# A planner that charges every load for the DMA queue, and weight clamps that GpSimd may take

## The chip, the cores and the metric

The kernel runs on one core of a Trainium2 chip. The metric is device time in microseconds (us), the median of several executions. A profile of one execution shows, for each engine, what it did and what it waited for: PE is TensorE's matmul side, PEld its weight loads, DVE is VectorE, ACT is ScalarE, POOL is GpSimd, and SP is SyncE, whose queue issues all of this kernel's loads and stores.

## The reference

Sliding-window attention for 8 batches of 8 heads (576 positions, head size 64, window 64) feeds an RWKV channel mix.

```python
scores = where(0 <= i - j < 64, (q @ k.T) / 8, -1e9)
x      = softmax(scores) @ v                       # heads side by side: (8, 576, 512)
xp     = x shifted by one position
xk, xr = mu_k*x + (1-mu_k)*xp, mu_r*x + (1-mu_r)*xp
k      = maximum(xk @ w_k, 0);  v = (k*k) @ w_v    # w_k 512x1024, w_v 1024x512
out    = sigmoid(xr @ w_r) * v                     # w_r 512x512
```

The three weight matrices arrive as 64-bit floats; x, q, k and v are 32-bit.

## The kernel before, in words

The 4608 rows (8 batches of 576 positions) are cut into 9 units u of 512 rows, and each unit has 4 attention groups, one for each pair of heads. Group g runs in three bursts on PE: `scores` (16 matmuls, which the trace records as 32), `flip` (8 transposes of the softmax weights) and `values` (16 matmuls, 32 in the trace). Between them stand, on other engines: `least` (DVE, 8 masked row minima per group), `exp` (ACT, 8), `shares` (DVE, the reciprocal row sums, tile `rs`), `scale` (four GpSimd instructions or one DVE instruction for each half), and copies out of PSUM (tiles `pt`, `xT`).

A unit's channel mix takes the 4 `xT` tiles. `mix` makes blends (DVE or ACT, tile `d`) and splits each into a high and a low part (tile `xs`; the low part by POOL or DVE). Then PE runs r units (48 matmuls `bank<-xs,ws`), k units (96 more of the same name) and v units (96 matmuls `bank<-ks,ws`). A product of two split numbers takes three matmuls of 128x512.

Before unit 0 can run, the weights are decoded: 20 chunks of 128x512 (4 of w_r, then 8 of w_k, then 8 of w_v). Each chunk takes one `sign` (ACT, `wt<-w`), one `clamp` (`wt<-wt`), three integer steps on DVE, `shift` (`bank<-wt`), `top` (`bank<-w,bank`) and `low` (`wt<-w,bank`), then `first_part` (ACT, `ws<-wt`) and `second_part` (POOL or DVE, `ws<-wt,ws`).

The order of all instructions is set at build time. Every step is a `Piece` with a key, a cost in ns, the pieces it needs, the buffers that it takes and one or more engines. `play` plays the pieces through by these costs: a free engine begins the ready piece with the lowest key. A piece is ready when what it needs is done and, on another engine, a further `lag` has passed. The order in which pieces begin is the order in which instructions are written out. On the chip each engine then runs its own list strictly in that order and waits wherever data are late. So the costs are never times of the run; they decide only the order.

`transfer` makes the piece of a load. At the start 38 loads without a `key` of their own are recorded: q, k and v of groups 0 to 3, the 20 weight chunks and the two mix vectors. They get a `lag` that grows with the bytes recorded so far. The loads of groups 4 and on have a key and a fixed `lag` of 2000 ns. Each transfer costs SP 60 ns in the play, however many DMAs it issues. Groups 2 and 3 hold their q and k in one tile `qks`, group 3 its v in `vs`.

Line 69 of the kernel is a helper that records every operation, so nearly all rows of the profile carry L69; the tiles tell the steps apart.

Of the kernel before, what the change touches and what calls it, by code (L numbers as in the profile page):

```python
# [14 lines left out]
ALU = mybir.AluOpType  # L15
PSUM = bass.MemoryType.PSUM

P = 128
# [6 lines left out]
UB = 8  # L25
NU = B * NB // UB
TU = UB * W
# [16 lines left out]
LINK = 80  # L44

HI_MIN = struct.unpack("<f", struct.pack("<I", 0x38000000))[0]
HI_MAX = struct.unpack("<f", struct.pack("<I", 0x47EFFE00))[0]
# [3 lines left out]
def attn_rwkv_kernel(ctx, tc, qT, kT, v2, mu_k, mu_r, w_k, w_v, w_r, out):  # L51
# [9 lines left out]
    class Engine:  # L61


        def __init__(self, engine):
            self.engine = engine
# [5 lines left out]
    pe, dve, sca, pool, dma = (Engine(e) for e in (nc.tensor, nc.vector, nc.scalar, nc.gpsimd, nc.sync))  # L71
    room = {"tmp": TB, "bank": 8, "m": 4, "bits": 1, "s": 2, "t": 2, "x": 1, "pr": 4, "sums": 4, "pt": 4, "xT": XB,
            "xs": SB, "r": R_BUFS, "qk": 2, "v": 3}
    pieces = []
# [7 lines left out]
    class Piece:  # L82


        def __init__(self, engine, key, cost, fn, needs=(), takes=(), uses=(), lag=LINK, spare=0, port=False):
            self.costs = engine if isinstance(engine, dict) else {engine: cost}
            self.home = next(iter(self.costs))
            self.engine, self.key, self.fn = None, key, fn
            self.needs = [p for p in needs if p is not None]
            self.takes, self.uses, self.lag, self.spare, self.port = list(takes), list(uses), lag, spare, port  # L90
            for hold in (*self.takes, *self.uses):
                hold.users.append(self)
            self.done = None
            pieces.append(self)

    def play():

        left, free, now, begun, port = {}, {}, 0, [], 0
        for n, p in enumerate(pieces):
            for e in p.costs:  # L100
                left.setdefault(e, []).append((p.key, n, p))
                free[e] = 0
        for e in left:
            left[e].sort(key=lambda x: (x[2].home != e, *x[:2]))
        users = {id(h): len(h.users) for p in pieces for h in p.takes}
        ends = []
        times = [0]
        while any(left.values()):
            assert times, [(e, [(p.key, p.fn.__name__) for _, _, p in ps[:4]]) for e, ps in left.items()]
            now = heapq.heappop(times)  # L110
            while ends and ends[0][0] <= now:
                _, _, p = heapq.heappop(ends)
                for hold in (*p.takes, *p.uses):
                    users[id(hold)] -= 1
                    if not users[id(hold)]:
                        room[hold.tag] += 1
            for e, ps in left.items():
                if free[e] > now:
                    continue
                for _, n, p in ps:  # L120
                    if not all(q.done is not None and q.done + (q.lag if q.engine != e else 30) <= now for q in p.needs):
                        continue
                    tags = [h.tag for h in p.takes]
                    if any(room[tag] < tags.count(tag) + (p.spare if tag == "m" else 0) for tag in set(tags)):
                        continue
                    locks = e == "POOL" or (e == "DVE" and p.port)
                    if locks and port > now:
                        continue
                    if p.home != e and max(free[p.home], now) + p.costs[p.home] < now + p.costs[e]:
                        continue  # L130
                    for o in p.costs:
                        left[o].remove((p.key, n, p))
                    for tag in tags:
                        room[tag] -= 1
                    p.engine = e
                    free[e] = p.done = now + p.costs[e]
                    if locks:
                        port = p.done
                    begun.append(p)
                    for at in (p.done, p.done + 30, p.done + p.lag):  # L140
                        heapq.heappush(times, at)
                    heapq.heappush(ends, (p.done + p.lag, n, p))
                    break
        return begun
# [5 lines left out]
        return 150 + 0.52 * n  # L150

    def act_ns(n):
        return 95 + 0.86 * n

    def pool_ns(n):
        return 195 + 2.1 * n
# [1 line left out]
    engines = {"DVE": dve, "POOL": pool}  # L158
# [63 lines left out]
    def decode(n, loaded):  # L222
        ws, _, i, c = chunks[n]
        key = DECODE[n]
        word, bits = Hold("tmp"), [Hold("bank"), Hold("bits")]

        def sign(e):
            words[n] = tmp.tile([P, WC], F32, name="wt", tag="tmp", bufs=TB)
            sca.activation(words[n], raw[n][:, :, 1].bitcast(F32), AF.Abs)

        def clamp(e):
            dve.tensor_scalar(words[n], words[n], HI_MIN, HI_MAX, op0=ALU.max, op1=ALU.min)

        def shift(e):
            words[n, 0] = bank(WC).bitcast(U32)
            dve.tensor_scalar(words[n, 0], words[n].bitcast(U32), 3, 0x3FFFFFF8,
                              op0=ALU.logical_shift_left, op1=ALU.bitwise_and)

        def top(e):
            dve.scalar_tensor_tensor(words[n, 0], raw[n][:, :, 1], 0xC0000000, words[n, 0],  # L240
                                     op0=ALU.bitwise_and, op1=ALU.bitwise_or)

        def low(e):
            dve.scalar_tensor_tensor(words[n].bitcast(U32), raw[n][:, :, 0], 29, words[n, 0],
                                     op0=ALU.logical_shift_right, op1=ALU.bitwise_or)

        def first_part(e):
            ws[i, c] = const.tile([P, 2, WC], F32R, name="ws", tag="w", bufs=len(chunks))
            sca.copy(ws[i, c][:, 0], words[n])

        def second_part(e):
            engines[e].tensor_sub(ws[i, c][:, 1], words[n], ws[i, c][:, 0].bitcast(F32))

        p = Piece("ACT", key, 600, sign, [loaded], takes=[word])
        p = Piece("DVE", key, 430, clamp, [p], port=True)
        p = Piece("DVE", key, 700, shift, [p], takes=bits)
        p = Piece("DVE", key, 700, top, [p])
        p = Piece("DVE", key, 700, low, [p], uses=bits)
        p0 = Piece("ACT", key, 560, first_part, [p])
        decoded[id(ws), i, c] = p0, Piece({"POOL": 1270, "DVE": 700}, key, 0, second_part, [p0], uses=[word], port=True)  # L260


    loaded, arrived, held = {}, {}, {}
    bus = [0]

    def transfer(fn, size, takes=(), needs=(), key=None):

        p = Piece("SP", len(pieces) - 9999 if key is None else key, 60, fn, needs, takes, lag=2000)
        if key is None:
            bus[0] = max(bus[0], 1300) + size / 300  # L270
            p.lag = bus[0] + 900
        return p


    groups = [(u, c) for u in range(NU) for c in range(NC)]
# [29 lines left out]
    def load_qk(g, key=None):  # L305
        u, c = groups[g]
        held[g] = [Hold("xs" if g in (2, 3) else "qk")]

        def load(e):
            if g in (2, 3):  # L310
                both = act.tile([P, 2, TU], F32, name="qks", tag="xs", bufs=SB)
                loaded[g] = [both[:, 0], both[:, 1]]
            else:
                loaded[g] = [ld.tile([P, TU], F32, name="q"), ld.tile([P, TU + 2 * W], F32, name="k")]
            q, k = loaded[g]
            for b, k0, k1, o in key_loads[u]:
                dma.dma_start(k[:, o * W:(o + k1 - k0) * W], kT[b * NP + c, :, k0 * W:k1 * W])
            o = 0
            for b, i0, i1 in stretches(u):
                n = i1 + 1 - i0  # L320
                dma.dma_start(q[:, o * W:(o + n) * W], qT[b * NP + c, :, i0 * W:(i1 + 1) * W])
                o += n

        arrived[g] = transfer(load, 4 * P * 2 * TU, held[g], key=key)

    def load_v(g, key=None):
        u, c = groups[g]
        held["v", g] = [Hold("xs" if g == 3 else "v")]

        def load(e):  # L330
            if g == 3:
                loaded["v", g] = act.tile([P, UB, P], F32, name="vs", tag="xs", bufs=SB)
            else:
                loaded["v", g] = ld.tile([P, UB, P], F32, name="v", bufs=3)
            for b, a, c0, c1, o in value_loads[u]:
                dma.dma_start(loaded["v", g][:, o:o + c1 - c0], v2[b * NP + c, :, a, c0:c1])

        arrived["v", g] = transfer(load, 4 * P * P * UB, held["v", g], key=key)

    banks, weights, sums, flipped = {}, {}, {}, {}  # L340
    xTs, got = {}, {}
# [316 lines left out]
    load_v(1)  # L658
    load_w(1)
    load_qk(3)  # L660
    arrived["mu"] = Piece("DVE", -25, 300, rest, [transfer(vectors, 4096)])
    load_v(2)
    load_w(1)
    load_v(3)
# [74 lines left out]
```

## Time and profile before

| What | Value |
| --- | --- |
| Median of 3 runs | 698.28 us (697.8 to 699.03) |
| The profiled execution | 697.61 us, of which the span is 695.8 us |
| PE busy | 633.5 us, 91% of the span |
| DVE busy | 413.8 us, 59% |
| ACT busy | 415.6 us, 60% |
| POOL busy | 112.8 us, 16% |
| Granted TensorE clock | 0.989 of full speed |

Shares of busy time are means over stages that differ much. The span has a start of some 130 us, in which weights are decoded and the first groups run, and a long part after it in which PE hardly ever waits. A step of the start is to be read in the start.

### The profile page before, as it was taken

Reading aid. Unit: us, or ns where it says so; the run is one execution under the profiler, and the core shown is the slowest. Engines: PE = TensorE matmul, PEld = TensorE weight load, DVE = VectorE, ACT = ScalarE, POOL = GpSimd, SP = SyncE. Lnnn points to the kernel's source line nnn. Section 1 sums busy time; section 2 is a strip of 40 time slices with the busy share of each in tenths; the row PEclk is TensorE's granted clock in tenths of the full one; section 3 lists DMA queues with packets and bytes.
Section 4 is the critical chain, followed back from the end, with each engine's and each line's share of the span. In section 5 each row is a group of like instructions: output and inputs, shape, how many; then the busy total and the mean of one; then the engine's idle time right before and its main releaser. Section 6 shows DMA issues by size and latency. Waiting matters only on the chain.

```text
span 695.8 us, 12937 instructions
## 1 busy us (share of the span) xinstructions
PE 633.5 (91%) x4752; PEld 510.0 (73%) x4752; DVE 413.8 (59%) x1194; ACT 415.6 (60%) x1130; POOL 112.8 (16%) x183
## 2 busy tenths in 40 slices
PE   1058687899999999999999999999999999999997
PEld 0036565787788888888888888888888888888886
DVE  1047999968758556754675467646764676353311
ACT  2049866947887368646754775477647764671540
POOL 2027784520001000200020002000200020000000
PEclk9998999999999999999999999999999999999999
DMA  8952200244122222222122123222322230001001
GB/s 316 401 183 84 56 1 0 72 151 134 59 60 90 90 60 59 90 90 61 59 90 90 60 59 105 76 65 65 114 80 71 67 112 29 1 16 45 1 0 61
DMA packets 47583, 57.87 MB, mean 83 GB/s; under 512 B 7584, under 2 KB 39328, under 8 KB 47520
## 3 DMA queue, kind: packets, MB, share of 16 engines
q1 hardware_dynamic: 47520, 57.04, 25.4%
q8 instruction: 38, 0.62, 0.4%
q14 instruction: 25, 0.20, 0.1%
HBM read 47.58 MB, written 9.44 MB: 82 GB/s over the span
## 4 chain that ended last, share of the span: by engine, by line
PE 79%; DVE 8%; DMA 5%; ACT 3%; issue 2%; POOL 1%; SPq 0%; DVEq 0%
PE bank L69 79%; DVE bank L69 3%; DVE wt L69 2%; DMA w<-w_v 2%; ACT pr L69 1%; DVE pr L69 1%; DMA q<-qT 1%; DMA w<-w_k 1%; DMA qks<-qT 1%; DMA v<-v 1%; DVE d L69 1%; POOL pr L69 1%; DVE r L69 1%; SPq L69 0%; ACT d L69 0%
## 5 line engine op out<-in xcount | busy, mean ns | idle before, releaser
L69 PE MATMUL bank<-xs,ws 128*128 128x512 f32 x1296 | 316.5, 400 | 9.3 <-ACT xs L69 3.5
L69 PEld LDWEIGHTS bank<-xs,ws 128*128 128x128 f32 x1296 | 244.1, 190 | 68.6 <-ACT xs L69 4.7
L69 PE MATMUL bank<-ks,ws 128*128 128x512 f32 x864 | 209.1, 396 | 1.7 <-ACT xT L69 1.7
L69 PEld LDWEIGHTS bank<-ks,ws 128*128 128x128 f32 x864 | 161.6, 188 | 38.8 <-ACT xT L69 2.1
L69 ACT ACTIVATE pr<-pr,nmax 128x128 f32<-128x128 f32 x288 | 111.9, 393 | 42.5 <-DVE nmax L69 42.4
L69 DVE TENSOR_TENSOR ks<-kf,ks 128x512 fp32r<-128x512 f32 x66 | 45.6, 692 | 82.3 <-ACT ks L69 81.0
L69 PE MATMUL bank<-k,q 64*64 64x128 f32 x1088 | 41.5, 289 | 40.0 <-DMA q<-qT 39.4
L69 ACT ACTIVATE kf<-bank 128x512 f32<-128x512 f32 x72 | 43.0, 599 | 48.6 <-PE bank L69 45.9
L69 PEld LDWEIGHTS bank<-k,q 64*64 64x64 f32 x1088 | 32.4, 140 | 52.3 <-DMA q<-qT 35.8
L69 ACT COPY xT<-bank 128x512 f32<-128x512 f32 x35 | 20.6, 588 | 77.0 <-PE bank L69 76.9
L69 DVE SCALAR_TENSOR_TENSOR r<-bank,r 128x512 f32<-128x512 f32 x36 | 24.9, 692 | 60.7 <-PE bank L69 60.6
L69 DVE CUSTOM_DVE_ANT_0 pr<-bank,maskNone 128x128 f32<-128x128 f32 x224 | 53.7, 286 | 10.5 <-PE bank L69 10.5
L69 ACT ACTIVATE th<-bank 128x512 f32<-128x512 f32 x36 | 21.5, 598 | 63.7 <-PE bank L69 59.6
L69 POOL TENSOR_SCALAR pr<-pr,rs 128x128 f32<-128x128 f32 x76 | 31.8, 437 | 162.8 <-ACT d L69 90.9
L69 ACT ACTIVATION_READ_ACCUMULATOR pr<-pr,nmax 128x1 f32 x288 | 54.9, 191 | 0.0
L69 POOL TENSOR_TENSOR kf<-kf 128x512 f32<-128x512 f32 x12 | 12.5, 1041 | 253.9 <-ACT kf L69 253.9
L69 PE MATMUL bank<-ident,pr 128*128 128x128 f32 x288 | 44.1, 290 | 6.1 <-POOL pr L69 3.3
L69 ACT CAST xs<-d 128x512 fp32r<-128x512 f32 x72 | 43.8, 618 | 3.7 <-DVE d L69 1.6
L69 ACT CAST ks<-kf 128x512 fp32r<-128x512 f32 x72 | 44.2, 617 | 1.7
L69 DVE CUSTOM_DVE_ANT_0 pr<-bank,mask 128x128 f32<-128x128 f32 x64 | 17.9, 286 | 44.3 <-PE bank L69 44.3
L69 PEld LDWEIGHTS bank<-pt,v 128*64 128x64 f32 x1120 | 37.2, 142 | 8.2 <-issue 5.5
L69 PE MATMUL bank<-pt,v 128*64 128x64 f32 x1120 | 42.3, 230 | 1.0 <-ACT kf L69 0.5
(54 smaller groups left out, 585.3 us busy)
## 6 DMA issues: line engine op xcount, KB each, us to landing
v<-v SPq DMA_DIRECT2D x31, 192.0 KB, 2.8
w<-w_k SPq DMA_DIRECT2D x8, 512.0 KB, 8.0
w<-w_v SPq DMA_DIRECT2D x8, 512.0 KB, 10.4
v<-v SPq DMA_DIRECT2D x32, 128.0 KB, 2.4
v<-v SPq DMA_DIRECT2D x15, 256.0 KB, 3.9
v<-v SPq DMA_DIRECT2D x36, 64.0 KB, 2.4
w<-w_r SPq DMA_DIRECT2D x4, 512.0 KB, 5.6
outT<-r SPq DMA_DIRECT2D x8, 256.0 KB, 2.0
```

The source lines that it names most:

```text
L69: return lambda *args, **kw: tc.keep_in_program_order(op(*args, **kw))
```

## The change

`play` now keeps the time until which the DMA queue is taken (`bus`). Every transfer, keyed or not, adds its bytes at 380 a ns when it begins, and its `lag` becomes the time until its bytes are through plus 2000 ns. A transfer costs SP 470 ns for each DMA that it issues. The fixed estimate of ACT's cost per column rises. `clamp` may be taken by POOL, where DVE would be done later, and it applies its upper limit first.

```diff
-        def __init__(self, engine, key, cost, fn, needs=(), takes=(), uses=(), lag=LINK, spare=0, port=False):
+        def __init__(self, engine, key, cost, fn, needs=(), takes=(), uses=(), lag=LINK, spare=0, port=False, size=0):
...
                     if locks:
                         port = p.done
+                    if p.size:
+                        bus = max(bus, p.done) + p.size / 380
+                        p.lag = bus - p.done + 2000
...
     def act_ns(n):
-        return 95 + 0.86 * n
+        return 95 + 0.94 * n
...
         def clamp(e):
-            dve.tensor_scalar(words[n], words[n], HI_MIN, HI_MAX, op0=ALU.max, op1=ALU.min)
+            engines[e].tensor_scalar(words[n], words[n], HI_MAX, HI_MIN, op0=ALU.min, op1=ALU.max)
...
-        p = Piece("DVE", key, 430, clamp, [p], port=True)
+        p = Piece({"DVE": 430, "POOL": 1000}, key, 0, clamp, [p], port=True)
...
-    bus = [0]
-
-    def transfer(fn, size, takes=(), needs=(), key=None):
-
-        p = Piece("SP", len(pieces) - 9999 if key is None else key, 60, fn, needs, takes, lag=2000)
-        if key is None:
-            bus[0] = max(bus[0], 1300) + size / 300
-            p.lag = bus[0] + 900
-        return p
+    def transfer(fn, size, takes=(), needs=(), key=None, dmas=1):
+
+        return Piece("SP", len(pieces) - 9999 if key is None else key, 470 * dmas, fn, needs, takes, size=size)
...
-        arrived[g] = transfer(load, 4 * P * 2 * TU, held[g], key=key)
+        arrived[g] = transfer(load, 4 * P * 2 * TU, held[g], key=key, dmas=2 * len(key_loads[u]))
...
-        arrived["v", g] = transfer(load, 4 * P * P * UB, held["v", g], key=key)
+        arrived["v", g] = transfer(load, 4 * P * P * UB, held["v", g], key=key, dmas=len(value_loads[u]))
```

What it does to the written order is seen at three places. The first is PE's list from its first matmul on. Loads signal on eight semaphores (DMAHW0 to DMAHW7) in turn, so that the pair that a `k,q` row waits for tells whose load it is: 1 and 0 are group 0's, 3 and 4 group 1's, 6, 7, 0 and 1 in the third row below are the four DMAs of group 4. Before:

```order
L69 MATMUL bank<-k,q 64x128 [waits DMAHW1_49,DMAHW0_49]
L69 MATMUL bank<-k,q 64x128 x15
L69 MATMUL bank<-k,q 64x128 [waits DMAHW6_49,DMAHW0_49]
L69 MATMUL bank<-k,q 64x128
L69 MATMUL bank<-k,q 64x128 [waits DMAHW7_49,DMAHW1_49]
L69 MATMUL bank<-k,q 64x128 x13
L69 MATMUL bank<-ident,pr 128x128 [waits Pool_49] x8
L69 MATMUL bank<-k,q 64x128 [waits DMAHW3_49,DMAHW4_49,DVE_49,PE_49]
```

The same place of PE's list now, by names alone (`qks` is group 2, then group 3, and the first row holds groups 0 and 1):

```order
L69 MATMUL bank<-k,q 64x128 x32
L69 MATMUL bank<-qks 64x128 x16
L69 MATMUL bank<-ident,pr 128x128 x8
L69 MATMUL bank<-pt,v 64x64 x16
L69 MATMUL bank<-qks 64x128 x16
```

Group 4's scores stood second on PE, ahead of the transposes of group 0 and of the scores of group 1; now groups 0, 1, 2 go first, and group 4's scores come after 45 `bank<-xs,ws` matmuls.

The second place is DVE's list behind the minima of group 0. Before, with buffer numbers (bank_227 and bank_228 are the scores of group 4, rs_212 the row sums of group 0, wt_259 weight chunk 0):

```order
L69 ISA pr_214,nmax_210<-bank_186,maskNone_78 128x128
L69 ISA nmax_210 128x1
L69 ISA pr_254,nmax_255<-bank_227,mask1_103 128x128
L69 ISA nmax_255 128x1
L69 ISA pr_261,nmax_255<-bank_228,mask1_103 128x128
L69 ISA nmax_255 128x1
L69 TENSOR_SCALAR rs_212<-sums_211 128x8
L69 RECIPROCAL rs_212<-rs_212 128x8
L69 TENSOR_SCALAR wt_259<-wt_259 128x512
```

And now (bank_183 and bank_184 are the scores of group 1, rs_161 is group 0's, wt_163 is chunk 0):

```order
L69 ISA pr_165,nmax_159<-bank_136,maskNone_78 128x128
L69 ISA nmax_159 128x1
L69 TENSOR_SCALAR wt_163<-wt_163 128x512
L69 TENSOR_SCALAR bank_201<-wt_163 128x512
L69 SCALAR_TENSOR_TENSOR bank_201<-w_121,bank_201 128x512
L69 ISA pr_213,nmax_214<-bank_183,mask0_92 128x128
L69 ISA nmax_214 128x1
L69 ISA pr_221,nmax_214<-bank_184,mask0_92 128x128
L69 ISA nmax_214 128x1
L69 TENSOR_SCALAR rs_161<-sums_160 128x8
L69 RECIPROCAL rs_161<-rs_161 128x8
```

The row sums of group 0 and the decode of chunk 0 stood behind group 4's minima, and now stand behind group 1's or ahead of them.

The third place is POOL's list in the middle of the decode, where five clamps (chunks 9 to 12 and 16 of 0 to 19) now stand. Before, there was none:

```order
L69 TENSOR_TENSOR ws_846<-wt_755,ws_846 128x512
L69 TENSOR_TENSOR ws_864<-wt_844,ws_864 128x512
L69 TENSOR_TENSOR ws_882<-wt_849,ws_882 128x512
L69 TENSOR_SCALAR pr_666<-pr_666,rs_669 128x128 x4
L69 TENSOR_SCALAR pr_710<-pr_710,rs_669 128x128 x4
```

Now three clamps precede a `second_part` (ws_806, chunk 7) and the scaling of group 4 (pr_728, pr_746):

```order
L69 TENSOR_TENSOR ws_743<-wt_688,ws_743 128x512
L69 TENSOR_SCALAR wt_736<-wt_736 128x512
L69 TENSOR_SCALAR wt_783<-wt_783 128x512
L69 TENSOR_SCALAR wt_789<-wt_789 128x512
L69 TENSOR_TENSOR ws_806<-wt_711,ws_806 128x512
L69 TENSOR_SCALAR pr_728<-pr_728,rs_731 128x128 x4
L69 TENSOR_SCALAR pr_746<-pr_746,rs_731 128x128 x4
```

On SP the first 42 DMAs keep their order (the last four are group 4's q and k); behind them the loads of groups 4 to 7 change places among themselves. From the row of 36 `bank<-xs,ws` matmuls in unit 1 on, PE's list reads the same as before, row for row, to its end.

More of the change, by code (lines that the diff above doesn't have):

```diff
@@ L89, in __init__ @@
             self.needs = [p for p in needs if p is not None]
-            self.takes, self.uses, self.lag, self.spare, self.port = list(takes), list(uses), lag, spare, port
+            self.takes, self.uses, self.lag, self.spare, self.port, self.size = list(takes), list(uses), lag, spare, port, size
             for hold in (*self.takes, *self.uses):
@@ L96, in play @@
     def play():
-        left, free, now, begun, port = {}, {}, 0, [], 0
+        left, free, now, begun, port, bus = {}, {}, 0, [], 0, 0
         for n, p in enumerate(pieces):
@@ L660, in attn_rwkv_kernel @@
     load_qk(3)
-    arrived["mu"] = Piece("DVE", -25, 300, rest, [transfer(vectors, 4096)])
+    arrived["mu"] = Piece("DVE", -25, 300, rest, [transfer(vectors, 4096, dmas=2)])
     load_v(2)
```

## The prediction

> **What bounds the kernel now.** I read the page first, then the chain that ended last, then the waits, then PE's and DVE's timelines of the start. From the page, engines in 40 slices of 17.4 us:
>
> ```profile
> span 695.8 us, 12937 instructions
> PE   1058687899999999999999999999999999999997
> DVE  1047999968758556754675467646764676353311
> ```
>
> PE is full from the ninth slice on and nearly idle in the first two. The chain, in order of time (start, length, what), with its lines of interest:
>
> ```profile
> 34.14 7.20 DMA q<-qT
> 41.38 2.49 PE bank L69 x32
> ...
> 127.25 31.39 PE bank L69 x278
> ...
> 181.18 510.90 PE bank L69 x3661
> ```
>
> It starts with loads until 41.38, goes through a decode stage in which most links are DVE's, and belongs to PE from 127.25 on. The waits of the whole run (us in total, times, longest) say what the first 41 us are:
>
> ```profile
> PE bank L69 <- DMA q<-qT: 39.4, 2, 35.2
> ACT pr L69 <- DVE nmax L69: 42.4, 6, 33.9
> POOL pr L69 <- DVE rs L69: 70.8, 5, 39.9
> ```
>
> One wait of PE for a load lasts 35.2 us, and the long waits of ACT and POOL stand behind it, since DVE's next minima need the scores that PE can't make. SP's and PE's timelines name the load:
>
> ```profile
> 2.59 0.43 SPq L69 DMA_DIRECT2D q<-qT  x1
> 34.14 1.58 SPq L69 DMA_DIRECT2D q<-qT  x2
> 4.22 1.98 PE L69 MATMUL bank<-k,q 64*64 64x128 f32 x32 [4.22 <-DMA q<-qT]
> 41.38 2.44 PE L69 MATMUL bank<-k,q 64*64 64x128 f32 x32 [35.18 <-DMA q<-qT]
> ```
>
> The second burst at 41.38 is group 4's, whose q was issued at 34.14 behind all 20 weight chunks; group 1's q was issued at 2.59.
>
> **The change part by part.** *Group 4's scores leave PE's second place.* The new second burst is group 1's. Time from issue to landing of the loads that now gate the start, from four one-DMA views (group 1's q, issued at 2.59; group 2's, 5.29; group 3's, 9.57; the second mix vector, 11.59):
>
> ```profile
> q<-qT SPq DMA_DIRECT2D x1, 256.0 KB, 5.8
> qks<-qT SPq DMA_DIRECT2D x1, 256.0 KB, 6.9
> qks<-qT SPq DMA_DIRECT2D x1, 256.0 KB, 6.4
> mur<-mu_r SPq DMA_DIRECT2D x1, 2.0 KB, 4.8
> ```
>
> They land at 8.4, 12.2, 16.0 and 16.4. SP issues these in the same order and at the same times as before, so PE's wait shrinks from 35.2 to about 2.2 us (6.2 to 8.4). That is 33 us at most for this wait alone; what counts is when DVE, the next bound, finishes the decode. Its share of the stage from 75.2 to 127.2, beside a stretch in which PE is the bound (busy us of PE, PEld, DVE, ACT, POOL):
>
> ```profile
> 75.20:127.20 52.00, 39.91 (x207) 28.84 (x204) 50.92 (x76) 37.83 (x72) 35.05 (x33) 0.93 0.05 14
> 480.00:540.00 60.00, 60.00 (x494) 48.98 (x493) 38.52 (x121) 36.57 (x105) 5.61 (x9) 1.00 0.26 80
> ```
>
> DVE is busy 50.92 of 52. Its first instruction of all, the first behind the stall and the last chunk's `low`:
>
> ```profile
> 6.36 0.29 DVE L69 CUSTOM_DVE_ANT_0 pr<-bank,mask 128x128 f32<-128x128 f32 x1 [6.36 <-PE bank L69]
> 43.96 0.29 DVE L69 CUSTOM_DVE_ANT_0 pr<-bank,mask 128x128 f32<-128x128 f32 x1 [35.82 <-PE bank L69]
> 131.62 0.64 DVE L69 SCALAR_TENSOR_TENSOR wt<-w,bank 128x512 uint32<-128x512 uint32 x1
> ```
>
> So 43.96 to 132.26, 88.3 us, is DVE's queue from the stall to the end of the decode. Now I count what the new list holds up to its last `low`, beginning with group 0 (DVE 6.36, right behind the burst of 4.22). Both have 48 minima in that stretch (before: groups 4, 1, 2, 3, 5, 6; now: 0 to 5), 20 shifts, tops and lows, 8 blends and 4 times three steps of `share`. They differ in clamps (20 before, 15 now), in 128x512 copies, scalings and subtractions (6 before, 10 now), and in one pair of row sums less. Prices are these groups from 75.2 to 132.3 (busy us, mean ns), and a clamp that nothing delayed:
>
> ```profile
> L69 DVE SCALAR_TENSOR_TENSOR bank<-w,bank 128x512 uint32<-128x512 uint32 x14 | 9.8, 696 | 0.5
> L69 DVE TENSOR_SCALAR bank<-wt 128x512 uint32<-128x512 uint32 x14 | 9.6, 684 | 0.0
> L69 DVE TENSOR_SCALAR wt<-wt 128x512 f32<-128x512 f32 x14 | 8.8, 658 | 0.0
> L69 DVE SCALAR_TENSOR_TENSOR r<-th,r 128x512 f32<-128x512 f32 x4 | 4.7, 1183 | 0.1
> L69 DVE COPY pt<-bank 128x512 f32<-128x512 f32 x1 | 0.7, 685 | 0.0
> L69 DVE RECIPROCAL rs<-rs 128x8 f32<-128x8 f32 x2 | 0.4, 203 | 0.1
> 44.71 0.38 DVE L69 TENSOR_SCALAR wt<-wt 128x512 f32<-128x512 f32 x1
> ```
>
> Minus 5 clamps at 0.38 to 0.66 (1.9 to 3.3), plus 4 steps at 0.69 (2.8), minus 0.4 for the row sums (two steps at the 0.2 of the reciprocal): between -0.9 and +0.5, so DVE's work is the same, 88 us. From 6.4 that ends at 94.7. To it comes idle time that the four start groups cause, since DVE can't decode far ahead there. Bounds: nothing, and 10 us, if DVE had nothing to do until the last of the four landings (16.4 - 6.4). Following the queue by hand gives about 4: 0.6 until group 1's burst is through, 1 before the row sums of group 1 (16 exponentials of ACT stand ahead), the rest before the copies of `xT` and group 3's minima. In return PE's, ACT's and POOL's part of each start group now lies beside DVE's decode less densely than before. I take 3: the decode ends at about 97.5 in place of 132.3, 34.8 earlier.
>
> *From the decode's end to the run's end.* From its row of 36 `xs` matmuls in unit 1, PE's list is the old one, so the gain is the difference in when PE gets there. PE's timeline shows the pace of the flow:
>
> ```profile
> 94.32 13.19 PE L69 MATMUL bank<-xs,ws 128*128 128x512 f32 x50 [0.20 <-POOL xs L69]
> 127.25 7.24 PE L69 MATMUL bank<-ks,ws 128*128 128x512 f32 x30 [1.66 <-ACT xT L69]
> 134.43 1.10 PE L69 MATMUL bank<-k,q 64*64 64x128 f32 x32
> 137.39 8.62 PE L69 MATMUL bank<-ks,ws 128*128 128x512 f32 x36
> ```
>
> A matmul is 0.24 us and an attention burst 2.96 (134.43 to 137.39). At 132.3 PE had done 21 `ks` matmuls. At the same point of the decode the new list has PE between 9 of them with group 6's burst still ahead (5.9 us behind before: 12 x 0.24 + 2.96) and 36 with that burst done (3.6 ahead), where it would have flowed since the k units. The last chunk stands behind 45 `ks` matmuls and two bursts, so it holds PE up less than in the old order. I take 1 behind: the gain is 34, and the bounds from the two terms are 34.8 - 7 - 5.9 = 22 and 34.8 + 3 + 3.6 = 41.
>
> *Clamps on POOL.* No row has a 512-column clamp there. Nearest: eight 128-column scalings undisturbed, and 512-column tensor steps.
>
> ```profile
> 45.01 2.81 POOL L69 TENSOR_SCALAR pr<-pr,rs 128x128 f32<-128x128 f32 x8 [39.94 <-DVE rs L69]
> L69 POOL TENSOR_TENSOR ws<-wt,ws 128x512 fp32r<-128x512 f32 x18 | 23.8, 1333 | 14.7 <-ACT ws L69 14.6
> L69 POOL TENSOR_TENSOR xs<-d,xs 128x512 fp32r<-128x512 f32 x10 | 14.4, 1450 | 15.2 <-ACT xs L69 10.5 <-DVE nmax L69 4.7
> ```
>
> The first gives 4 x 0.35 = 1.4 as an upper bound for 512 columns, or 0.35, should most of it be start-up, as the lower. I take 1.3, like the first of the equally long rows. Five are 6.5 us on an engine with 35.05 of 52 busy in that stage; queued behind the first three are chunk 7's `second_part` and the scaling of group 4, on which PE waits. The cover is the k units' backlog; if it's gone, some 4 us come through, which the lower end above takes in. A rule speaks against this part. The Trainium skill (GPSIMD Engine Reference, "4.1 Engine selection") sends an elementwise max to VectorE and not to GpSimd, and its "1. Specifications" says that GpSimd shares SBUF interfaces with VectorE. The trace agrees as far as it goes: steps that write or read PSUM keep 684 to 696 ns in the table above while the SBUF-only clamp goes from 380 to 658 and `r<-th,r` to 1183. By this rule, with all of POOL's 6.5 us taken out of DVE's time and the clamps' 1.9 saved there, the time would be 664 + 6.5 - 1.9 = 669, on the way to rival A.
>
> *Costs of ACT, order of later loads.* Nothing: they act on the plan alone, and in 480 to 540 PE is busy 60.00 of 60.00 with DVE at 38.52 and ACT at 36.57. If that cover were gone, a wait would show there; I allow 2 us.
>
> The sum: 697.61 of the profiled execution minus 34 is 663.6; the median of the runs lies 0.67 higher, so 664.
>
> **The rivals.** *A, the plan takes part of it back (like the forecast, but smaller).* POOL's extra 6.5 us stretch DVE's SBUF-only steps. In 75.2 to 132.3 those already lost, against undisturbed durations, 14 x 0.28 for clamps and 4 x 0.49 for `r<-th,r`, 5.9 us with the two largest groups alone. If that doubles (6), the idle start time is the full 10 (7 more) and PE is 5.9 behind, 34.8 - 6 - 7 - 5.9 = 16 remain: 682. For it speaks that DVE is the bound there; against it, that all must come together.
>
> *B, another load takes the place of the one removed.* The last chunk's buffer now waits until chunk 0 is decoded, and group 4's loads stand behind it on SP, which reached that DMA here:
>
> ```profile
> 30.40 0.33 SPq L69 DMA_DIRECT2D w<-w_v  x1
> ```
>
> Each us by which it leaves later moves group 4's landing (34.14 + 7.20 = 41.3) back as much. PE now comes to that group's scores behind four start groups (the last q lands at 16.0, and they took PE from 41.4 to 75.2 before) and 45 `xs` matmuls (10.8 us), at about 45. So 4 us of delay cost nothing and 20 cost 16: 680. Against it: chunk 0's `low` is DVE's 38th row in the new list, behind two groups' minima, some 7 us after its first.
>
> *C, the change doesn't do what it says.* If the landing of group 1's q were itself bound to the weights behind it, PE would wait to about 41 again: 698. The 5.8 us row contradicts it, unless the profiled execution was lucky.
>
> *D, slower: GpSimd's min and max are far slower than its multiply.* Five clamps in the path of chunks 9 to 12 and 16 and of group 4's scaling give up the gain of 34 if each takes 34/5 = 6.8 us more than 1.3. At 10 us each the time would be 697.6 - 34 + 5 x 8.7 = 707. Against it stand the rows above, 0.35 for 128 columns and 1.33 and 1.45 for 512.
>
> **How the numbers follow.** The forecast, a gain of 22 to 41 us (657 to 676, most likely 664), gets 0.76; more than 41, if DVE's delays beside POOL shrink in the new order, 0.06; A 0.12; B 0.02; C 0.02; D 0.02. The range for 8 in 10 is 655 to 678: it takes in the bounds, the 2 us of the steady part, and the near side of A. What a measurement can tell from no change is about 0.2%, 1.4 us. Faster: 0.76 + 0.06 + 0.12 + 0.02 = 0.96; same: C, 0.02; slower: D, 0.02.
>
> **What would show it.** Right: PE's second burst at about 8.4 us behind a wait of 2 us for a load, the last `wt<-w,bank` on DVE at 95 to 100, PE without waits from then on, and five `wt<-wt` on POOL near 1.3 us each. Wrong by A: DVE's SBUF-only means above 0.8 us for clamps and the last `low` beyond 105. Wrong by B or C: a PE wait for a DMA of over 10 us. Wrong by D: a POOL clamp above 3 us with `bank<-ident,pr` waiting for POOL. A steady stretch with PE below 59 of 60 would refute the claim that the later order costs nothing. I would be most surprised by an early start whose gain is lost between 50 and 100 us.

## The result and the profile after

The changed kernel takes 661.45 us (median of four executions, 660.5 to 662.79), the kernel before 698.23 beside it: a ratio of 0.9473 (95% interval 0.9455 to 0.9492), 36.8 us less. The execution that was profiled took 662.79 us, with a span of 661.0. It is the slowest of the four, and the one of before (697.61) is quicker than the four runs of that kernel beside it (697.8 to 699.03), so the two traces differ by 34.8 us of span, 2 us less than the medians.

The page after, the same rows as before (40 slices, now of 16.5 us):

```profile
span 661.0 us, 12919 instructions
PE   4875989999999999999999999999999999999997
DVE  4899987795676467546755675558554766273311
```

The two nearly empty slices at the head are gone, and PE is full from the seventh slice on in place of the ninth. In the chain, PE's last link starts at 133.15 (before 181.18):

```profile
133.15 524.06 PE bank L69 x3769
```

PE's timeline after, rows that waited and the rows that the prediction named:

```profile
8.49 1.98 PE L69 MATMUL bank<-k,q 64*64 64x128 f32 x32 [2.34 <-DMA q<-qT]
12.19 1.98 PE L69 MATMUL bank<-qks 64*64 64x128 f32 x32 [1.72 <-DMA qks<-qT]
50.77 1.70 PE L69 MATMUL bank<-k,q 64*64 64x128 f32 x30 [4.06 <-DVE wt L69]
58.11 1.62 PE L69 MATMUL bank<-xs,ws 128*128 128x512 f32 x3 [5.65 <-DVE nmax L69]
85.04 0.94 PE L69 MATMUL bank<-ks,ws 128*128 128x512 f32 x3 [1.24 <-ACT kf L69]
92.09 8.62 PE L69 MATMUL bank<-ks,ws 128*128 128x512 f32 x36
133.15 1.02 PE L69 MATMUL bank<-ident,pr 128*128 128x128 f32 x4 [1.84 <-DVE pr L69]
133.82 9.98 PE L69 MATMUL bank<-xs,ws 128*128 128x512 f32 x36
```

The wait of 35.18 is one of 2.34. Behind the loads of the first groups, what PE waits for up to 92 is mostly VectorE. The last row is the place in unit 1 from which both lists read alike. In the kernel before it stands here:

```profile
169.12 8.62 PE L69 MATMUL bank<-xs,ws 128*128 128x512 f32 x36
```

So PE is there 35.3 us earlier (169.12 - 133.82), and from there to the end both take the same: 526.7 before (695.8 - 169.12), 527.2 now. The whole difference is made ahead of this row. Two more views after, DVE's last `low` and the windows (busy us of PE, PEld, DVE, ACT, POOL, then granted clock, DMA share and GB/s):

```profile
94.23 0.69 DVE L69 SCALAR_TENSOR_TENSOR wt<-w,bank 128x512 uint32<-128x512 uint32 x1
```

```profile
6.32:94.92 88.60, 69.20 (x565) 53.79 (x566) 79.92 (x216) 72.59 (x192) 59.95 (x79) 0.92 0.54 198
440.00:500.00 60.00, 60.00 (x435) 48.92 (x434) 37.42 (x106) 36.36 (x100) 6.46 (x11) 1.00 0.24 74
```

The first window is DVE's stretch from its first instruction to the end of the last `low`. The same stretch before, from behind the stall:

```profile
43.96:132.26 88.30, 70.45 (x534) 52.13 (x535) 83.51 (x219) 71.88 (x191) 60.12 (x81) 0.92 0.17 48
```

The stretch is as long as it was, with 3.6 us less work in it and 3.9 us more idle time. The clamps after, on both engines, up to 110 us:

```profile
L69 DVE TENSOR_SCALAR wt<-wt 128x512 f32<-128x512 f32 x15 | 8.7, 595 | 0.0
L69 POOL TENSOR_SCALAR wt<-wt 128x512 f32<-128x512 f32 x5 | 3.4, 679 | 0.3
```

### The profile page after: what moved, and what is told of

It reads as the page before. It is cut to its first block, busy times and chain, and to the rows that moved or that the text cites. A ratio compares the mean times of both kernels' runs of the same rounds, so it can differ in the third digit from the quotient of the medians.

```text
span 661.0 us, 12919 instructions
## 1 busy us (share of the span) xinstructions
PE 631.5 (96%) x4752; PEld 511.1 (77%) x4752; DVE 409.0 (62%) x1193; ACT 412.8 (62%) x1122; POOL 118.5 (18%) x186
## 4 chain that ended last, share of the span: by engine, by line
PE 87%; DVE 5%; ACT 3%; issue 2%; DMA 1%; SPq 1%; POOL 0%; ACTq 0%; DVEq 0%; POOLq 0%
PE bank L69 87%; DVE bank L69 2%; DVE wt L69 1%; DMA qks<-qT 1%; ACT pr L69 1%; DVE r L69 1%; ACT d L69 1%; SPq L69 1%; ACT kf L69 0%; DVE pr L69 0%; DVE d L69 0%; ACT pt L69 0%; ACT ws L69 0%; ACT wt L69 0%; POOL xs L69 0%
## 5 line engine op out<-in xcount | busy, mean ns | idle before, releaser
L69 POOL TENSOR_TENSOR xs<-d,xs 128x512 fp32r<-128x512 f32 x14 | 27.8, 1987 | 79.6 <-ACT xs L69 79.6
L69 POOL TENSOR_SCALAR pr<-pr,rs 128x128 f32<-128x128 f32 x68 | 28.5, 441 | 60.9 <-ACT d L69 50.2
```

Of the source, the lines that this page charges most:

```text
L69: return lambda *args, **kw: tc.keep_in_program_order(op(*args, **kw))
```

## The experiments

The result leaves four questions. Is it the wait for the load alone, or also the new order? Does it need the model of the queue? What are the five clamps on GpSimd worth? Does ACT's cost matter? The ratios, each against the kernel before on the same chip:

| Kernel | Median us | Ratio (95%) |
| --- | --- | --- |
| changed kernel | 661.45 | 0.9473 (0.9455 to 0.9492) |
| its clamps planned on VectorE | 667.12 | 0.9549 (0.9535 to 0.9564) |
| its plan, clamps issued by VectorE | 666.86 | 0.9566 (0.954 to 0.9591) |
| before, clamp choice alone | 696.34 | 0.9965 (0.9951 to 0.998) |
| before, group 4 late in the plan | 699.21 | 1.0011 (1.0 to 1.0023) |
| before, all keyed loads late in the plan | 666.3 | 0.9547 (0.9533 to 0.9561) |
| before's order, group 4's load early | 678.73 | 0.9714 (0.9696 to 0.9732) |
| before's order, group 4's and 5's early | 667.99 | 0.9576 (0.9563 to 0.959) |
| changed, old ACT cost | 660.07 | 0.9465 (0.945 to 0.9479) |
| changed, GpSimd clamp priced 650 | 660.74 | 0.9467 (0.9454 to 0.948) |
| changed, both of these | 661.17 | 0.947 (0.945 to 0.949) |
| changed, three prices nearer to the trace | 660.11 | 0.9462 (0.9443 to 0.9482) |
| changed, all 20 clamps on GpSimd | 667.5 | 0.9557 (0.9541 to 0.9572) |

**The load alone, by hand.** The order of every compute engine stays that of before; on SP's list group 4's q and k move up behind the second weight chunk. (`first`, group 0's scores, moves with them in the written list and stays at the head of PE's own.)

```diff
+    order = play()
+    first, early = next(p for p in order if p.engine == "PE"), arrived[4]
+    order = [p for p in order if p is not first and p is not early]
+    place = order.index([p for p in order if p.engine == "SP"][4]) + 1
+    order[place:place] = [first, early]
```

> The kernel before, with the same order on PE, VectorE, ScalarE and GpSimd; only the four DMAs of group 4's q and k are moved ahead of the weights on SP, behind the second weight chunk. Theory (the load is late, and nothing else in the order is bad): group 4's burst at about 12 us in place of 41, a new wait of some 5 us for group 5's load, 665 to 675 us. Rival (the order of the start is bad in itself, and the new order is what helps): 685 us or more.

It took 678.73, between the two. PE's timeline:

```profile
12.06 2.53 PE L69 MATMUL bank<-k,q 64*64 64x128 f32 x32 [5.89 <-DMA q<-qT]
45.52 2.45 PE L69 MATMUL bank<-k,q 64*64 64x128 f32 x32 [8.38 <-DMA q<-qT]
```

The first wait fell from 35.18 to 5.89 us, and the next group's load, still behind the weights, took 8.38 back. That left open whether the old order has a price of its own. So group 5's q and k were moved as well:

```diff
+    order = [p for p in order if p is not arrived[5]]
+    place = order.index([p for p in order if p.engine == "SP"][12]) + 1
+    order[place:place] = [arrived[5]]
```

> The kernel before, with every compute engine's list as it was; on SyncE's list group 4's q and k stand behind the second weight chunk and group 5's behind the second mix vector. With group 4's alone moved it took 678.7, with a new wait of 8.4 us for group 5's load. Theory (the loads' waits are all that was wrong with the old order; clamps stay on VectorE, so the mark is the 667 of the changed kernel without clamps on GpSimd): 665 to 671, and no wait of PE for a load above 4 us behind the first burst but group 4's own 6 us. Rival (the old order also costs in itself, by its early row minima or later k units): 674 or more, though the wait for group 5 is gone.

It took 667.99. PE's timeline and DVE's last `low`:

```profile
12.22 2.45 PE L69 MATMUL bank<-k,q 64*64 64x128 f32 x32 [6.01 <-DMA q<-qT]
36.85 1.34 PE L69 MATMUL bank<-k,q 64*64 64x128 f32 x32
139.49 8.62 PE L69 MATMUL bank<-xs,ws 128*128 128x512 f32 x36
```

```profile
101.97 0.64 DVE L69 SCALAR_TENSOR_TENSOR wt<-w,bank 128x512 uint32<-128x512 uint32 x1
```

Group 5's burst at 36.85 waits no more, and the `xs` row of unit 1 comes 29.6 us earlier than before (169.12 - 139.49). The theory holds: with no row of PE, DVE, ACT or POOL moved, the two loads give 30.1 us of the 36.8.

**The plan, told in another way.** First only group 4's load was made late in the play of the kernel before, in place of all loads:

```diff
         arrived[g] = transfer(load, 4 * P * 2 * TU, held[g], key=key)
+        if g == 4:
+            arrived[g].lag = 44000
```

> The kernel before with one number changed: in the plan group 4's load arrives 44 us after it begins. Group 5's load keeps its 2 us, and its scores now stand third on PE. Theory (any burst whose load stands behind the weights stalls PE): PE waits some 30 us for group 5's load and the time is 688 to 702 us. Rival (group 4's place alone): 662 to 670 us.

No gain, as the theory had it: group 5's scores took the place, and PE waited for their load:

```profile
43.30 2.47 PE L69 MATMUL bank<-k,q 64*64 64x128 f32 x32 [33.41 <-DMA q<-qT]
```

Then every load with a key was told to land at 44 us or later, with nothing else of the change:

```diff
+                    if e == "SP" and p.lag == 2000:
+                        p.lag = max(2000, 44000 - p.done)
```

> The kernel before (old costs, no clamp on GpSimd, no model of the queue), in which every load with a key is told to land at 44 us or later in the play; group 4's load alone, so told, had left 699. Theory (what pays is that the planner stops putting groups whose loads are late ahead of work that is ready; the model of the queue is one way to get there, and five clamps on GpSimd are worth some 5 us on top): the wait of 35 us is gone, 662 to 671, about the 667 of the changed kernel with its clamps on VectorE. Rival (the bytes and issue times of the queue's model are needed for a good order): a wait for a load of 8 us or more stays and the time is 678 or more.

666.3 us. One constant in the right place did as much as the bytes and issue times of the queue's model (667.12 with the model and no clamp on GpSimd). PE's largest wait for a load behind its first burst is gone here too: all waits of PE for `q<-qT` are 7.0 us, the first burst's 4 us among them.

**The clamps.** The changed kernel with the clamp bound to VectorE in the plan:

```diff
-        p = Piece({"DVE": 430, "POOL": 1000}, key, 0, clamp, [p], port=True)
+        p = Piece("DVE", key, 430, clamp, [p], port=True)
```

> The planned loads and the new ACT cost, but all 20 clamps on VectorE. Theory (the late load is the cause): PE's second burst again at about 8.5 us, 662 to 666 us, at most 4 us above the changed kernel. Rival (the clamps on GpSimd carry a good part): 668 us or more.

PE's second burst stood at 8.75. 667.12 is just past the theory's range and short of the rival's: the clamps on GpSimd carry 5.3 us (0.0076 of 698; with both intervals, about 3.6 to 7). The other way round, the clamp's choice was put into the kernel before:

```diff
-            dve.tensor_scalar(words[n], words[n], HI_MIN, HI_MAX, op0=ALU.max, op1=ALU.min)
+            engines[e].tensor_scalar(words[n], words[n], HI_MAX, HI_MIN, op0=ALU.min, op1=ALU.max)
...
-        p = Piece("DVE", key, 430, clamp, [p], port=True)
+        p = Piece({"DVE": 430, "POOL": 1000}, key, 0, clamp, [p], port=True)
```

> The kernel before with clamps that GpSimd may take, loads planned as before. Theory: the 35 us wait stays, 694 to 699 us. Rival (clamps): 690 us or less.

696.34, with the long wait in place. In this plan GpSimd took only one clamp, so the run does not say what five would bring in the old order:

```profile
42.19 2.45 PE L69 MATMUL bank<-k,q 64*64 64x128 f32 x32 [36.03 <-DMA q<-qT]
```

A plan with the clamps elsewhere also has another order, so the two were parted: the changed kernel's plan, in which VectorE issues the five clamps at the same places.

```diff
-            engines[e].tensor_scalar(words[n], words[n], HI_MAX, HI_MIN, op0=ALU.min, op1=ALU.max)
+            dve.tensor_scalar(words[n], words[n], HI_MAX, HI_MIN, op0=ALU.min, op1=ALU.max)
```

> The changed kernel's plan as it is (same order on TensorE, ScalarE and of all other steps), but the five clamps that the plan gave to GpSimd are issued by VectorE at the same places of the order. It parts the clamps' own work from the new order that their planning brings (planned on VectorE they cost 5.3 us: 667.1). Theory 1 (VectorE sets the decode's end, so the work itself counts: 5 clamps at 0.38 to 0.66 us): 663 to 665. Theory 2 (the order counts, the five clamps' work is hidden): 660.5 to 662.5. Theory 3 (GpSimd's reading and writing beside VectorE costs as much as it saves, so without it the time is lower): under 660.5.

666.86: the order is not it (theory 2 falls), nor does GpSimd's work cost what it saves (theory 3 falls), and the work is worth more than theory 1 said (5.4 us by the medians, 6.5 by the ratios). DVE's clamps, its stretch to the last `low`, and PE's rows:

```profile
L69 DVE TENSOR_SCALAR wt<-wt 128x512 f32<-128x512 f32 x20 | 12.6, 642 | 0.2 <-ACT wt L69 0.2
```

```profile
6.32:97.23 90.91, 67.77 (x562) 51.88 (x563) 84.46 (x221) 72.53 (x192) 57.22 (x74) 0.91 0.52 188
```

```profile
58.09 1.62 PE L69 MATMUL bank<-xs,ws 128*128 128x512 f32 x3 [7.26 <-DVE nmax L69]
87.68 0.93 PE L69 MATMUL bank<-ks,ws 128*128 128x512 f32 x3 [3.05 <-DVE wt L69]
```

DVE has 84.46 us of work in place of 79.92, of which the clamps are 3.9 (12.6 - 8.7). Its decode ends 2.3 us later (97.23 against 94.92), and PE's waits for it grow from 5.65 to 7.26 and, at 87.68, to 3.05 where it had waited 1.24 for ACT; another wait for DVE, 4.06 at 50.77 in the changed kernel, is 2.95 here. Over the whole run PE is idle 4.1 us longer (33.6 against 29.5) and busy 0.8 less (630.7 against 631.5), which makes the 3.3 between the spans (664.3 and 661.0). The other 2 us of the medians' 5.4 come from where the profiled executions lie: this one is 0.8 below its median, the changed kernel's 1.3 above.

Five clamps at 0.42 us, which is what most of VectorE's clamps take in these traces, would be 2.1 us and not 4.5. The rest is steps of VectorE that were held up. Three lines of this run:

```profile
53.43 0.42 DVE L69 TENSOR_SCALAR wt<-wt 128x512 f32<-128x512 f32 x1
55.38 1.26 POOL L69 TENSOR_TENSOR ws<-wt,ws 128x512 fp32r<-128x512 f32 x1 [3.89 <-ACT ws L69]
55.47 1.46 DVE L69 TENSOR_SCALAR wt<-wt 128x512 f32<-128x512 f32 x1
```

The second clamp began 0.09 us after a GpSimd `second_part` and ended 0.29 us behind it (56.93 against 56.64). Four of this run's 20 clamps and one of its four `th<-th` before 97 us were held for about as long and took 1.46 to 1.53 us; in the changed kernel it was two of 15 clamps and no `th<-th`. So a mean of 595 or 642 ns is mostly a mix of 0.42 and 1.5 us. Whether the clamps on GpSimd bring fewer such meetings by more than the chance of one order was not tried.

How far this goes was tried with the old ACT cost, with a lower price on GpSimd (650 ns, near the trace's rows), with both, and with the new ACT cost again and GpSimd's and VectorE's tensor steps priced nearer to the trace. The edits are, in this order, the second, the first, the first two, and the first with the last two:

```diff
-        p = Piece({"DVE": 430, "POOL": 1000}, key, 0, clamp, [p], port=True)
+        p = Piece({"DVE": 430, "POOL": 650}, key, 0, clamp, [p], port=True)
...
-        return 95 + 0.94 * n
+        return 95 + 0.86 * n
...
-        return 150 + 0.52 * n
+        return 150 + 0.45 * n
...
-        return 195 + 2.1 * n
+        return 195 + 2.2 * n
```

> The changed kernel with the planner's old cost of ACT (0.86 a column instead of 0.94); five clamps still stand on GpSimd, and rows change places. Theory (ACT's cost is nothing by itself): 659 to 664, within 2.5 us of the changed kernel's 661.4. Rival (the higher cost of ACT keeps ACT's and VectorE's work balanced in the decode): 665 or more.

> The changed kernel with GpSimd's clamp priced at 650 in the play, as the trace has it (0.62 us), instead of 1000: eight clamps on GpSimd instead of five. Theory (VectorE sets the end of the decode, and each clamp that it loses is worth about 1 us, as five were worth 5.3): 657 to 660. Rival (GpSimd, 41.88 us busy of 51 in the decode, delays the second parts and scalings behind its clamps): 661 to 666.

> The changed kernel with both the clamp's price of 650 on GpSimd and the old ACT cost; alone these gave 660.7 and 660.1. Theory (each is noise of the order by about 1 us, and nothing adds up, since VectorE's decode is full in all of them): 659 to 663. Rival (their gains add up): 658 or less.

> The changed kernel with three of the planner's prices nearer to the trace's rows (clamp on GpSimd 650, GpSimd's tensor steps 195 + 2.2 a column, VectorE's 150 + 0.45 a column). Theory (after the loads' times are right, the plan's prices are worth a few us either way): 658 to 665. Rival (truer prices give a better order in the decode): 656 or less.

All four lie at 660.1 to 661.2, and their intervals overlap the changed kernel's. ACT's cost makes no difference that can be measured, as expected. Eight or nine clamps on GpSimd are worth no more than five: 660.74 lies between the two theories' ranges, and the theory that each further clamp brings 1 us falls. None of these beats the changed kernel by what can be measured. Last, all 20:

```diff
-        p = Piece({"DVE": 430, "POOL": 1000}, key, 0, clamp, [p], port=True)
+        p = Piece("POOL", key, 650, clamp, [p], port=True)
```

> The changed kernel with all 20 clamps on GpSimd at a price of 650. Theory (each clamp off VectorE is worth about 1 us as long as GpSimd has room; 15 more are 9.3 us of GpSimd at 0.62 us): if there is room, 646 to 655. Rival (GpSimd fills up in the decode and each clamp then holds up shift, top and low behind it): 660 to 670, with VectorE waiting for GpSimd at rows of the shift.

667.5, the rival. The decode's windows, and what DVE's shift waited for up to 110 us:

```profile
47.00:98.00 51.00, 38.86 (x283) 29.32 (x282) 42.37 (x116) 40.87 (x107) 43.72 (x60) 0.86 0.26 77
```

```profile
L69 DVE TENSOR_SCALAR bank<-wt 128x512 uint32<-128x512 uint32 x20 | 13.8, 688 | 9.1 <-ACT kf L69 5.1 <-POOL wt L69 4.1
102.29 0.69 DVE L69 SCALAR_TENSOR_TENSOR wt<-w,bank 128x512 uint32<-128x512 uint32 x1
```

Now POOL is busier than DVE (43.72 against 42.37), DVE waits 4.1 us for GpSimd's clamps and 5.1 for ACT, and the last `low` ends 8 us later than in the changed kernel. In this plan GpSimd also does all 72 low parts of `xs` (14 in the changed kernel), so not all of the loss need be the clamps'.

## Why the prediction was right, point by point

**The bound and the stall: right.** The second burst stood at 8.49 behind a wait of 2.34 us (8.4 and 2.2 foreseen), and the two loads that block the old order are 30.1 us by themselves. What the prediction did not see is that the old order has two such loads: group 5's would have cost 8.4 us if only group 4's had come early. In the new order neither waits, so nothing hung on it.

**DVE's stretch: the idle time right, the work mis-sized.** The sum said equal work (bounds -0.9 to +0.5) and 3 us more idle time, an end at 97.5. Measured: idle time 3.9 more (8.7 against 4.8), but work 3.6 us less, an end at 94.92. The term that failed is the work. Its two largest counted parts came out: the clamps are 2.6 us less (11.3 - 8.7), and the ten copies, scalings and subtractions take 2.6 more than the six did, with 2.8 foreseen. But the sum carried the old durations of all other steps over to the new list, and some steps that touch SBUF alone became shorter in the mean. Groups of DVE over the whole stretch, before and after:

```profile
L69 DVE TENSOR_SCALAR th<-th 128x512 uint32<-128x512 uint32 x4 | 2.8, 696 | 0.0
L69 DVE SCALAR_TENSOR_TENSOR r<-th,r 128x512 f32<-128x512 f32 x4 | 4.7, 1183 | 0.1
L69 DVE TENSOR_SCALAR wt<-wt 128x512 f32<-128x512 f32 x20 | 11.3, 591 | 0.0
```

```profile
L69 DVE TENSOR_SCALAR th<-th 128x512 uint32<-128x512 uint32 x4 | 1.7, 414 | 0.0
L69 DVE SCALAR_TENSOR_TENSOR r<-th,r 128x512 f32<-128x512 f32 x4 | 3.8, 940 | 0.1
```

The single rows say why: before, one of the four `th<-th` and two of the four `r<-th,r` were held behind a GpSimd step (1.53, and 1.67 and 1.68 us), now none and one. The others took 0.41 to 0.42 and 0.69 in both. The clamps, 591 ns in the mean of all 20 before and 595 of 15 now, did not become shorter: three of 20 and two of 15 were held. The 658 that the prediction showed is the mean of the 14 in its window; it read it as a stretch of every clamp.

**From the decode's end on: right, but for one wait.** "1 behind" was 2.0: DVE's end is 37.3 us earlier (132.26 - 94.92) and the common row 35.3. At 94.92 PE had done 9 `ks` matmuls, group 6's burst and 12 more (2.83 us at 0.24), level with the old order. The 2 us were lost behind it. PE waits 1.5 us longer than the old order did on the same work (2.0 against 0.45), nearly all of it at 133.15, 1.84 us for DVE's scaling of `pr`, which the prediction excluded ("PE without waits from then on"); and PE is busy 0.5 us longer. The gain in the profiled executions was 34.8, with 34 foreseen. That the two are so close is in part luck: the decode ended 2.5 us earlier than foreseen (37.3 for 34.8), and 1.5 of that were lost again behind it. The medians' gain of 36.8 is 2.8 above the forecast.

**The clamps on POOL: wrong in size.** They were taken at 1.3 us and took 0.68 in the mean, in the lower half of the bounds 0.35 and 1.4: the tensor steps, after which 1.3 was chosen, were the wrong row. What they bring was counted as 1.9 to 3.3 us less on DVE, hidden in a sum near 0. DVE's clamps are 2.6 us less than before (11.3 - 8.7) and 3.9 less than in the same plan without GpSimd, and the time is 5.3 to 6.5 shorter for them by the ratios. The prediction's own row, DVE 50.92 of 52, said that work taken off DVE counts there.

The other result, 669, by which GpSimd would stretch VectorE, is refuted: in the same plan without the five clamps on GpSimd the time is longer, not shorter, and `r<-th,r` takes 930 ns there against 940 with them. GpSimd does hold VectorE up, as the lines at 55.38 and 55.47 show, but its five clamps did not add to that. The Trainium skill (GPSIMD Engine Reference, "4.1 Engine selection") does send an elementwise max to VectorE, but the same row adds that with one input GpSimd is roughly at line rate. This trace agrees with the addition roughly: most clamps take 0.62 us there against 0.42 on VectorE, and the means of the stage are 0.68 and 0.60, in a kernel where VectorE was the full engine. The choice then goes by which engine has room there.

**ACT's cost and the later order: right.** PE is 60.00 of 60.00 busy in 440 to 500, and the old cost gives 660.07.

**The rivals.** A, a part given back by contention, did not come: of DVE's clamps, `th<-th` and `r<-th,r`, three were held behind GpSimd in the stretch, and six before. B, another load late, is what happened to the two half measures (33.41 and 8.38 us), not to the change. C is excluded by the 2.34 us, D by the 0.68.

## What to carry to other kernels

Where a planner writes the order of in-order queues, a load believed to be early puts the work that needs it at the head of a queue, and everything behind waits; correcting one such load moves the stall to the next, so all loads of the kind must be told late (here one crude constant did as well as a model of the queue). Which engine should take a small step is read from the stage's busy times: moving five clamps off the full engine paid 5 us although their new home is no faster, moving eight paid no more, and with all 20 moved the gain was lost again and the new home was the busier engine. A mean duration is worth taking apart by single rows before it goes into a sum: 0.6 us here was 0.42 for most steps and 1.5 for a few that stood behind another engine.

## What the runs showed of the chip beside this

The two kernels with loads moved by hand have the same PE list, yet PE is busy for 637.2 us in the one and 632.3 in the other. The windows of the start, first of group 4's load early, then of both:

```profile
47.00:98.00 51.00, 42.24 (x213) 31.76 (x205) 44.70 (x80) 32.94 (x68) 30.29 (x29) 0.80 0.11 37
```

```profile
47.00:98.00 51.00, 39.23 (x201) 28.51 (x201) 49.92 (x77) 36.60 (x70) 34.64 (x33) 0.93 0.16 50
```

The granted clock in 47 to 98 us was 0.80 in the one, behind a pause of 8.4 us, and 0.93 in the other; over the whole run it was 0.977 to 0.982 in each of four executions of the first and 0.989 to 0.992 in each of five of the second. The two ran on different chips, but the kernel before had 0.987 to 0.993 beside both. So 4.9 of the 11.8 us between their spans (678.0 and 666.2) are matmuls that took longer, not waits. The lower clock of the first began inside its pause (37.1 to 45.5) and outlasted it:

```profile
40.20:60.50 20.30, 12.85 (x114) 10.39 (x115) 8.84 (x30) 9.01 (x23) 6.26 (x12) 0.50 0.57 191
```

That the pause caused it is likely but was not tried by itself.
